# A second late projection with seven block products instead of eight, and an output stored transposed

## The chip, the cores and the metric

The kernel runs on one core of a Trainium2 chip. Its time is the device time of one execution in microseconds (us); of the kernel before, three executions took 549.82, 550.81 and 551.61 us, with a median of 550.81 us. The core has five engines, each with its own queue of instructions: TensorE (PE in the profile) multiplies matrices and writes to PSUM, an accumulator memory of eight banks; VectorE (DVE) and ScalarE (ACT) work on elements and read PSUM; GpSimd (POOL) works on SBUF, the working memory of 128 partitions; SyncE (SP) issues DMAs.

## The reference

A causal attention with a memory term, of 32 heads (4 x 8) with 576 positions of 64 values, gives x, 2304 tokens of 512 values. Then comes a feed-forward block, which is what the change touches:

```python
def _moe_ref(x, w_in, w_out):      # x 2304x512, w_in 512x2048, w_out 2048x512
    h = x @ w_in
    sp = np.where(h > 20.0, h, np.log1p(np.exp(np.minimum(h, 20.0))))
    g = h * np.tanh(sp)
    return (g @ w_out).astype(np.float32)
```

All is float32. The kernel gets that precision from a TensorE format that keeps fewer bits by splitting each operand into a high half (a rounded copy, made by ACT) and a low half (the rest, made by DVE), and by summing three products: high x high, high x low and low x high.

## The kernel before

The 2048 hidden values are cut into 16 units of 128. Units 0 to 3 (KA = 4) are done early: the tokens come in blocks of 512 as soon as a batch's attention is ready, and their first projection (`slot_h`, line 706) and second projection (`out_a`, line 734) fill gaps of TensorE between attention matmuls. Their sum goes to a DRAM tensor `part`.

Units 4 to 15 are done late, after attention. They form six pairs, in two groups of three (line 939). The tokens form three blocks of 768 (2 x HB). For each group and each block there is one late stage, so there are six stages, and each has two parts.

The first part is the first projection (`products`, line 807). A pair's 256 hidden values, a block's two halves of 384 tokens, and the two halves of the 512 inputs make a 2x2 by 2x2 block product, and that is done with seven block products instead of eight, on sums and differences of blocks (`factors`, line 758, for x; `split7`, line 430, for the weights). Each of the seven is 6 matmuls of 384 columns, so a stage has 3 x 7 x 6 = 126. The seven land in seven PSUM banks; DVE adds them up through four tiles `u` in SBUF. Then come the activation (Mish, ACT, in place in PSUM), the high half (ACT) and the low half (DVE), in a tile that the profile calls `xg`.

The second part is the second projection (`outputs`, line 862), a plain product: for each of 6 groups of 128 tokens, the 6 units of the group with 3 matmuls each of 512 columns, 108 in all, with the tokens as the weights of the systolic array. DVE adds `part` to each of the six banks, and SP stores the sum: to `part2` in the first group, to the output in the second.

The order of every engine's instructions is fixed when the program is built. A planner (`Plan`, `pick` at line 222) runs a list of operations through a model of the engines, with a priority for each operation, rings of buffers, and limits (`HELD`) on how many PSUM banks each kind of work may hold; the instructions are then issued in the order that it found, and each engine keeps to it. All instructions go through one helper, line 314, so that the tile's name, not the line, tells operations apart. [...]

Of the kernel before, what the change touches and what calls it, by code (L numbers as in the profile page):

```python
# [31 lines left out]
KA = 4  # L32
# [42 lines left out]
KEPT = {"raw": 2, "ca": 1, "cs": 2, "ob": 3}  # L75
MORE = {"ca": 2, "cs": 1, "ob": 1}
LATE = {"wi7": 3, "xT": 7, "xt": 3, "u": 5}
LANES = 8
HELD = {"ffn": 2, "att": 6, "tail": 8, "acc": 4, "conv": 1}
# [19 lines left out]

def f32(ap):  # L100
    return ap.bitcast(F32)


class Ring:


    def __init__(self, name, n):
        self.name, self.free, self.made, self.opened = name, [(0.0, k) for k in range(n)], 0, 0
        self.size, self.heirs, self.moves = n, [], None
# [9 lines left out]
class Op:  # L119
    __slots__ = ("eng", "dur", "fn", "prio", "kind", "bufs", "deps", "outs", "missing", "ready", "start", "end", "n", "kb", "tail", "port")  # L120


class Plan:


    def __init__(self):
        self.ops, self.writer, self.readers = [], {}, {}
        self.rings, self.held = {}, {"ffn": 0, "att": 0, "tail": 0, "acc": 0, "conv": 0}
# [4 lines left out]
    def op(self, eng, dur, fn, prio, r=(), w=(), bufs=(), kind=None, kb=0, port=False):  # L133
        o = Op()
        o.port = port or eng == "POOL"
# [23 lines left out]
    def opens(self, o):  # L159
# [5 lines left out]
        for ring, bs in need.items():  # L165
# [4 lines left out]
            if k:  # L170
                limit = HELD[k]
                if k == "att" and self.ffn_on:
                    limit = HELD["att"]
                elif k == "att":
                    limit = 8
                if self.held[k] + len(bs) > limit:
                    return None
        return t

    def place(self, o, start):  # L180
        o.start, o.end = start, start + o.dur
        if o.tail and not self.grown:
            self.grown = True
            for name, n in MORE.items():
                ring = self.rings[name]
                ring.free += [(o.end, ring.size + k) for k in range(n)]
        done = o.end + LAT[o.eng]
        if o.eng == "SP":
# [10 lines left out]
        for b in o.bufs:  # L199
            b.left -= 1  # L200
            b.end = max(b.end, done)
            if b.left == 0:
                ring = b.ring
                if ring.moves and ring.opened == ring.made:
                    ring = ring.moves
                ring.free.append((b.end, b.slot))
                ring.free.sort()
                if ring.heirs and ring.opened == ring.made and len(ring.free) == ring.size:
                    for heir, slots, others in ring.heirs:
                        if all(r.opened == r.made and len(r.free) == r.size for r in others):  # L210
                            t = max(r.free[-1][0] for r in others)
                            heir.free += [(t, k) for k in slots]
                            heir.free.sort()
                if b.kind:
                    self.held[b.kind] -= 1
        for x in o.outs:
            x.missing -= 1
            x.ready = max(x.ready, done if x.eng != o.eng or o.eng == "SP" else o.end + SAME[o.eng])
# [76 lines left out]
TABLE = 288.75  # L295


@with_exitstack
def attention_moe_kernel(ctx: ExitStack, tc: tile.TileContext, f_src, qn, vn, zz, beta, w_in, w_out, out):
# [4 lines left out]
    class Queue:  # L304
# [5 lines left out]
        def __getattr__(self, what):  # L310
            f = getattr(self._eng, what)

            def call(*a, **kw):
# [25 lines left out]
    part = dram.tile([NT, DM], F32, name="part")  # L339
    part2 = dram.tile([NT, DM], F32, name="part2")  # L340
# [4 lines left out]
             "ob": [128, 512], "raw": [128, 1024], "ca": [128, 512], "cs": [128, 512]}  # L345
# [8 lines left out]
    ident = sb.tile([128, 128], F32, name="ident")  # L354
    mask = sb.tile([128, 448], F32, name="mask")
    gt = sb.tile([128, 3, H], F32, name="gt")
    wt = [sb.tile([128, 4, 512], F32R, name=f"wt{f}") for f in range(KA)]
    xg = sb.tile([128, 10 * 1024], F32, name="xg")
    for name, n in (("x", 4), ("g", 6), ("g2", 0), ("wa", 2 * KA), ("wo", 0), *((r, n) for r, n in LATE.items())):
# [3 lines left out]
    slot["g2"] = [xg[:, 768 * k:768 * k + 768] for k in range(13)]  # L363
    slot["wa"] = slot["wo"] = [wt[k // 2][:, 2 * (k % 2):2 * (k % 2) + 2] for k in range(2 * KA)]
    x_, g_, g2_ = (P.rings[n] for n in ("x", "g", "g2"))
    x_.heirs = [(g2_, range(5), [x_]), (g2_, range(5, 13), [x_, g_])]
    g_.heirs = [(g2_, range(5, 13), [x_, g_])]
    P.rings["wa"].moves = P.rings["wo"]
    for name, n in KEPT.items():
        P.rings[name] = Ring(name, n)  # L370
        slot[name] = [sb.tile(SHAPE[name], F32, name=f"{name}{k}") for k in range(n)]
    attp = held.enter_context(tc.tile_pool(name="att", bufs=1))
    zall = attp.tile([128, NP * 2 * D], F32, name="zall")
# [3 lines left out]
    WA, WO7, WI7 = {}, {}, {}  # L377
# [4 lines left out]
    def tail_tiles():  # L382
        held.close()
        pool = ctx.enter_context(tc.tile_pool(name="tail", bufs=1))
        for name, shape, dt in (("wi7", [128, 2, 7 * 256], F32R), ("xT", [128, 4, HB], F32R), ("xt", [128, 2 * HB], F32),
                                ("u", [128, HB], F32)):
            slot[name] = [pool.tile(shape, dt, name=f"{name}{k}") for k in range(LATE[name])]
        for name, n in MORE.items():
            slot[name] += [pool.tile(SHAPE[name], F32, name=f"{name}m{k}") for k in range(n)]

# [33 lines left out]
    def split(f, k, prio):  # L424
        a, key = word(f, k, prio)
        wb = P.buf("wa" if f < KA else "wo")
        (WA if f < KA else WO7)[f, k] = wb
        halves(lambda: at(a), lambda i: at(wb)[:, i], 512, prio, [key + ("a",)], key, [a, wb], f >= KA)

    def split7(q, prio):  # L430

        f = KA + 2 * q
        wb = P.buf("wi7")
        WI7[q] = wb
        a, ka = word(f, 0, prio)
        halves(lambda: at(a), lambda i: at(wb)[:, i, 0:512], 512, prio, [ka + ("a",)], ("d", q, 0), [a, wb], True)
        b, kb = word(f + 1, 0, prio)
        halves(lambda: at(b)[:, 256:512], lambda i: at(wb)[:, i, 512:768], 256, prio, [kb + ("a",)], ("d", q, 1), [b, wb], True)
        t = P.buf("raw")
        tt = lambda i: at(t)[:, 256 * i:256 * i + 256]  # L440
        for i, (x, y, op) in enumerate(((lambda: at(b)[:, 0:256], lambda: at(b)[:, 256:512], ALU.add),
# [586 lines left out]
```

## Time and profile before

| what | value |
|---|---|
| median of three executions | 550.81 us (549.82 to 551.61) |
| the profiled execution, span from first to last instruction | 549.8 us (the page gives no other time of it; the fastest of the three is 549.82) |
| TensorE busy | 531.4 us, 97% |
| VectorE busy | 430.8 us, 78% |
| ScalarE busy | 337.0 us, 61% |
| GpSimd busy | 177.9 us, 32% |
| granted TensorE clock, mean | 0.996 of full speed |

A row of the profile names an engine, an operation, the tiles it writes and reads (written <- read), the shape, how many there were, and the busy time; behind that stands the idle time in front of it and who ended it. A busy time of several instructions counts overlaps once, while the mean of one is its full recorded length; so the distance between two starts can be shorter than the recorded length.

### The profile page before, as it was taken

The page shows a single profiled execution, that of the slowest core. Times are in us where ns is not written, and L with a number is a line of the kernel's source. Part 1 is how long each engine was busy: PE and PEld are TensorE (multiplying, and loading weights), DVE is VectorE, ACT ScalarE, POOL GpSimd, SP SyncE. Part 2 cuts the span into 40 slices and gives each one's busy share as a digit, 9 for nine tenths or more (in the row PEclk, how much of TensorE's full clock was granted, in tenths as well). Part 3 has the DMA queues.
Part 4 walks back from the last instruction along what each step waited for, and adds up shares of the span by engine and source line. Part 5 has one row for each costly group of instructions (what it writes and reads, how often), then busy time and mean ns, then how long its engine had stood idle before and what let it go on. Part 6 is the DMA issues. An engine that isn't in the chain of part 4 may idle for free.

```text
span 549.8 us, 10439 instructions
## 1 busy us (share of the span) xinstructions
PE 531.4 (97%) x3705; PEld 439.9 (80%) x3705; DVE 430.8 (78%) x1042; ACT 337.0 (61%) x804; POOL 177.9 (32%) x272
## 2 busy tenths in 40 slices
PE   5998999999999999999999999999999999999997
PEld 2665666777777777888998898889889889989985
DVE  4999999987898962786799779759899956864712
ACT  4999899998899774575785155417548404412500
POOL 1787787758776770011321100010212000000000
PEclk9899999999999999999999999999999999999999
DMA  7677584974566534965783914177385362534003
GB/s 254 241 258 244 169 269 154 297 291 123 160 205 185 187 118 144 385 221 170 223 253 114 301 50 170 58 241 237 115 276 181 120 221 67 173 98 132 0 19 134
DMA packets 48211, 99.77 MB, mean 181 GB/s; under 512 B 4000, under 2 KB 17824, under 8 KB 48160
## 3 DMA queue, kind: packets, MB, share of 16 engines
q1 hardware_dynamic: 48160, 99.11, 54.5%
q8 instruction: 29, 0.48, 0.4%
q14 instruction: 22, 0.18, 0.1%
HBM read 73.40 MB, written 23.59 MB: 176 GB/s over the span
## 4 chain that ended last, share of the span: by engine, by line
PE 84%; DVE 6%; DMA 3%; ACT 3%; POOL 2%; SPq 1%; issue 1%
PE bank L314 84%; DMA f<-in_f_src_dram 2%; DVE w L314 2%; ACT w L314 2%; DMA xT<-xs 1%; POOL w L314 1%; DVE at L314 1%; SPq L314 1%; DVE den L314 1%; DVE qn L314 1%; DVE xo L314 0%; ACT at L314 0%; ACT bank L314 0%; POOL phe L314 0%; DVE ca L314 0%
## 5 line engine op out<-in xcount | busy, mean ns | idle before, releaser
L314 PE MATMUL bank<-wt,xg 128*128 128x512 f32 x864 | 200.2, 391 | 0.0
L314 PEld LDWEIGHTS bank<-wt,xg 128*128 128x128 f32 x864 | 161.5, 188 | 33.7 <-issue 0.4
L314 PE MATMUL bank<-xT,wi 128*128 128x384 f32 x756 | 133.4, 335 | 0.7 <-DMA xT<-xs 0.7
L314 PEld LDWEIGHTS bank<-xT,wi 128*128 128x128 f32 x756 | 131.4, 188 | 1.8 <-DVE xg L314 1.0
L314 ACT ACTIVATE w<-w,mx 128x320 f32<-128x320 f32 (+4 forms) x160 | 88.7, 558 | 3.5 <-DVE mx L314 2.9
L314 POOL TENSOR_SCALAR w<-w,rc 128x320 f32<-128x320 f32 (+4 forms) x152 | 81.8, 562 | 13.9 <-DVE rc L314 4.3
L314 ACT ACTIVATE bank<-bank 128x384 f32<-128x384 f32 (+2 forms) x92 | 45.0, 495 | 56.1 <-DVE bank L314 51.8
L314 PE MATMUL bank<-f 64*128 64x288 f32 (+4 forms) x384 | 59.4, 425 | 8.3 <-DMA f<-in_f_src_dram 7.1
L314 DVE CUSTOM_DVE_ANT_0 w<-bank,mask 128x320 f32<-128x320 f32 (+4 forms) x160 | 60.2, 422 | 5.9 <-PE bank L314 5.9
L314 DVE TENSOR_TENSOR xg<-bank,xg 128x384 fp32r<-128x384 f32 (+2 forms) x92 | 50.1, 567 | 11.8 <-ACT xg L314 11.7
L314 PEld LDWEIGHTS bank<-f 64*128 64x128 f32 x384 | 38.7, 196 | 22.9 <-DMA f<-in_f_src_dram 7.9
L314 PE MATMUL bank<-at,v 128*64 128x256 f32 (+2 forms) x512 | 54.1, 363 | 0.0
L314 PE MATMUL bank<-xg,wt 128*128 128x512 f32 (+1 forms) x240 | 53.4, 375 | 0.6 <-ACT at L314 0.3
L314 PEld LDWEIGHTS bank<-at,v 128*64 128x64 f32 x512 | 34.2, 137 | 21.3 <-issue 2.0
L314 PEld LDWEIGHTS bank<-xg,wt 128*128 128x128 f32 x240 | 40.9, 188 | 9.8 <-issue 1.2
L314 POOL TENSOR_TENSOR cam<-cam,cs 128x512 int32<-128x512 int32 x13 | 17.5, 1346 | 95.5 <-ACT cs L314 34.2
L314 PEld LDWEIGHTS bank<-ident,w 64*128 64x128 f32 x928 | 35.0, 139 | 13.8 <-POOL w L314 5.7
L314 PE MATMUL bank<-ident,w 64*128 64x64 f32 x928 | 40.2, 226 | 5.0 <-ACT w L314 1.4
L314 ACT CAST xg<-bank 128x384 fp32r<-128x384 f32 (+2 forms) x92 | 43.8, 502 | 0.9
L314 DVE TENSOR_TENSOR ob<-bank,ob 128x512 f32<-128x512 f32 x27 | 18.3, 686 | 30.1 <-PE bank L314 27.1
L314 DVE TENSOR_TENSOR bank<-u,bank 128x384 f32<-128x384 f32 x72 | 38.5, 556 | 4.2 <-PE bank L314 3.8
L314 DVE COPY at<-bank 128x448 f32<-128x448 f32 x64 | 38.9, 641 | 1.9 <-PE bank L314 1.6
(76 smaller groups left out, 578.4 us busy)
## 6 DMA issues: line engine op xcount, KB each, us to landing
xT<-xs SPq DMA_DIRECT2D x18, 768.0 KB, 6.6
xs<-xo SPq DMA_DIRECT2D x16, 576.0 KB, 3.9
f<-in_f_src_dram SPq DMA_DIRECT2D x15, 576.0 KB, 4.9
raw<-in_w_in_dram SPq DMA_DIRECT2D x16, 512.0 KB, 4.6
raw<-in_w_out_dram SPq DMA_DIRECT2D x16, 512.0 KB, 4.2
part<-ob SPq DMA_DIRECT2D x29, 256.0 KB, 3.8
xg<-xs SPq DMA_DIRECT2D x14, 512.0 KB, 6.0
ob<-part SPq DMA_DIRECT2D x27, 256.0 KB, 3.9
```

Source lines behind the costliest of these rows:

```text
L314: ins = f(*a, **kw)
```

## The change

The second projection of the late units takes the same form as the first. A pair's 256 hidden values, a block's two token halves and the two halves of the 512 outputs again form a 2x2 by 2x2 product, done by seven block products (`STEPS`). The result is transposed: output values on partitions, tokens on columns, with matmuls of 384 columns and w_out as the array's weights. So `part` and the output are held as 128 x 4 x 2304 and 512 x 2304 (the early `out_a` is transposed too, with the same number of columns), and the caller transposes what it gets.

Both projections now share banks: three banks for the seven products of a pair (`more=True` goes on adding in a bank), six for the seven output products of a stage, which are summed over the three pairs. ACT copies partial sums out (`keep`), DVE adds them. The activation writes to SBUF (`g1`); `cuts` makes the seven factors of the second projection there, in place, one after another, and splits each in halves (`gf`, seven buffers). In the first group the result is added to `part` by a DMA that accumulates, issued from GpSimd; in the second group `part` is loaded, added and stored. An output tile has five buffers for eight uses in a stage. The weights of the second projection go through `split7` as well. The second group takes the token blocks in the order 2, 0, 1, and its first stage uses the x factors that the first group's last stage has left. The planner gets a table of one priority for each operation instead of rules; two lines of it stand in the diff.

```diff
-LATE = {"wi7": 3, "xT": 7, "xt": 3, "u": 5}
+LATE = {"wi7": 3, "xT": 7}
+SIDE = {(("t", 0, k), n) for k in (1, 2) for n in ("22", "21")}
+STEPS = [1, 5, 2, 6, 3, 7, 4]
-HELD = {"ffn": 2, "att": 6, "tail": 8, "acc": 4, "conv": 1}
+HELD = {"ffn": 2, "att": 6, "tail": 5, "acc": 6, "conv": 1, "gf": 7}
+LOW = 3
+FREE = 4
...
+PRIO = [
+    -419.6, 290.3, -717.2, -661.6, -1029.7, 165.8, 0.5, -337.1, -1035.4, 620.2, 77.7, 165.6, 28.1, 179.5, -812.2, -110.8, 185.3, -672.1, 41.5, -709.2, -12.2,
...
-    def split7(q, prio):
+    def split7(q, k, prio):
...
+        wb = P.buf("wo7" if k else "wi7")
+        W7[q, k] = wb
+        a, ka = word(f, k, prio)
...
         mm(1, "a11", "11")
...
+        keep(0, 1)
         mm(5, "s1", "t1")
...
+        keep(1, 5)
+        mm(2, "a12", "21", opens="11")
+        add(0, 2)
+        mish(2, "11")
+        mm(1, "s2", "t2", True)
+        keep(2, 1)
+        mm(5, "s4", "22", True, "12")
+        add(2, 5)
+        mish(5, "12")
+        mm(1, "s3", "t3", True, "22")
+        add(1, 1, "22")
+        mish(None, "22")
+        mm(1, "a22", "t4", True, "21")
+        mish(1, "21")
...
+    def cuts(qs, tag, prio, GT):
...
+        for i, n in enumerate(STEPS):
+            for q in qs:
+                gb, src = GT[q], FROM[n]
...
+                if n in (5, 6, 7, 4):
+                    pre(*{5: ("12", "11"), 6: ("22", "11"), 7: ("22", "12"), 4: ("21", "11")}[n])
+                b = P.buf("gf", "gf")
...
+                P.op("ACT", HB / 1200.0 + 0.09, lambda gb=gb, src=src, view=view: ac.copy(out=view(0), in_=at(gb[src])), when(prio + 3 * i),
...
+                P.op("DVE", HB / 960.0 + 0.075, lambda gb=gb, src=src, view=view: ve.tensor_tensor(out=view(1), in0=at(gb[src]), in1=f32(view(0)), op=ALU.subtract),
...
     def outputs
...
+        def store(a, b, c):
+            cc, ts = spot(a, b, c)
+            if not last:
...
+                P.op("POOL", SWDGE[0], lambda: po.dma_start(out=part[:, cc, ts], in_=at(pb[a, b, c]), accum_op=ALU.add), when(prio + 30),
...
+        for step, n, what in ((1, 1, [(0, 0, 0)]), (5, 5, [(1, 1, 0)]), (2, 2, [(0, 0, 1)]), (6, 1, [(0, 1, 0)]), (3, 5, [(0, 1, 1)]),
+                              (7, 1, [(1, 1, 1)]), (4, 1, [(1, 0, 1)])):
+            for c in range(2):
+                mm(step, n, c)
+            for c in range(2):
+                for a, b, end in what:
+                    if (a, b, c) not in pb:
+                        fetch(a, b, c, n)
+                    else:
+                        add(a, b, c, n)
+                    if end:
+                        store(a, b, c)
...
+        for k in ((0, 1, 2), (2, 0, 1))[gi]:
...
+            X, got = kept if gi and k == 2 else factors(k, tag, when(base - (45 if k == gi == 0 else 30)), gi)
```

On TensorE, at the place in the last stage where the second projection begins, the queue of before reads as follows (`wt0` to `wt3` hold the halves of w_out, `xg` those of the hidden values; behind a tile's name stand its buffer and a running number):

```order
L314 MATMUL bank5_72<-wt2_80,xg_82 128x512 x3
L314 MATMUL bank0_67<-wt2_80,xg_82 128x512 x3
L314 MATMUL bank1_68<-wt2_80,xg_82 128x512 x3
L314 MATMUL bank4_71<-wt2_80,xg_82 128x512 x3
L314 MATMUL bank5_72<-wt3_81,xg_82 128x512 x3
L314 MATMUL bank0_67<-wt3_81,xg_82 128x512 x3
```

There the changed queue has this, with the factors `gf`, the weights `wo7` of the three pairs, and the last product of the first projection (`xT`) in between:

```order
L475 MATMUL bank6_72<-gf2_3344,wo70_2860 128x384 x3
L475 MATMUL bank7_73<-gf2_3344,wo70_2860 128x384 x3
L475 MATMUL bank0_66<-gf3_3345,wo71_3340 128x384 x3
L475 MATMUL bank1_67<-xT6_2859,wi72_2852 128x384 x6
L475 MATMUL bank4_70<-gf3_3345,wo71_3340 128x384 x3
L475 MATMUL bank2_68<-gf0_3342,wo72_3341 128x384 x3
```

The 108 matmuls of 512 columns have become 126 of 384, and each three of them need a factor that one ACT and one DVE instruction have made.

On VectorE, one pair's share of a late stage before (adds of products through `u`, then low halves into `xg`):

```order
L314 TENSOR_TENSOR u0_2878<-u3_2881,bank1_68 128x384
L314 TENSOR_TENSOR u4_2882<-u0_2878,bank5_72 128x384
L314 TENSOR_TENSOR bank4_71<-u3_2881,bank4_71 128x384
L314 TENSOR_TENSOR u1_2879<-u0_2878,bank6_73 128x384
L314 TENSOR_TENSOR bank6_73<-u4_2882,bank6_73 128x384
L314 TENSOR_TENSOR bank7_74<-u4_2882,bank7_74 128x384
L314 TENSOR_TENSOR xg_82<-bank4_71,xg_82 128x384
L314 TENSOR_TENSOR bank2_69<-u1_2879,bank2_69 128x384
L314 TENSOR_TENSOR xg_82<-bank6_73,xg_82 128x384
L314 TENSOR_TENSOR xg_82<-bank7_74,xg_82 128x384
L314 TENSOR_TENSOR xg_82<-bank2_69,xg_82 128x384
```

The same place in the last stage of the changed queue (`g1` with its buffer behind it, so `g12` is buffer 2, holds the hidden values and in place the differences, `gf` the halves):

```order
L475 TENSOR_TENSOR bank4_70<-u2_3362,bank4_70 128x384
L475 TENSOR_TENSOR g11_3350<-u1_3361,bank3_69 128x384
L475 TENSOR_TENSOR g16_3355<-g12_3351,g16_3355 128x384
L475 TENSOR_TENSOR g12_3351<-g11_3350,g12_3351 128x384
L475 TENSOR_TENSOR gf5_3347<-g16_3355,gf5_3347 128x384
L475 TENSOR_TENSOR g16_3355<-g11_3350,g16_3355 128x384
L475 TENSOR_TENSOR gf1_3343<-g11_3350,gf1_3343 128x384
L475 TENSOR_TENSOR gf6_3348<-g19_3358,gf6_3348 128x384
L475 TENSOR_TENSOR bank7_73<-u0_2861,bank7_73 128x384
L475 TENSOR_TENSOR g19_3358<-g19_3358,g16_3355 128x384
L475 TENSOR_TENSOR bank6_72<-u2_3362,bank6_72 128x384
```

Ten instructions for a pair (6 adds, 4 low halves) have become 14 (3 adds, 4 differences, 7 low halves), and those of several pairs stand mixed.

On GpSimd, in the second and third late stage, the changed queue has the new accumulating stores between the instructions that assemble weights:

```order
L475 DMA part_65<-oo_81 128x384 x5
L475 DMA part_65<-ot0_2862 128x384
L475 TENSOR_TENSOR xt_2864<-xt_2864,cs1_86 128x512
L475 TENSOR_TENSOR xt_2864<-xt_2864,cs0_85 128x512
L475 DMA part_65<-oo_81 128x384 x2
```

Before, GpSimd has only the assembling instructions there.

## Rows read from the trace of the kernel before

**Rows 1.** The page: the span, and busy time (share) x instructions.
```profile
span 549.8 us, 10439 instructions
PE 531.4 (97%) x3705; PEld 439.9 (80%) x3705; DVE 430.8 (78%) x1042; ACT 337.0 (61%) x804; POOL 177.9 (32%) x272
```

**Rows 2.** Chain of waits, its end: start, length, what.
```profile
329.69 6.74 DMA xT<-xs
336.56 209.45 PE bank L314 x1038
546.04 0.69 DVE ob L314
```

**Rows 3.** Timeline of TensorE, fifth stage and on: start, length, instructions.
```profile
453.06 22.03 PE L314 MATMUL bank<-xT,wi 128*128 128x384 f32 x126
474.93 24.68 PE L314 MATMUL bank<-wt,xg 128*128 128x512 f32 x108
499.45 22.03 PE L314 MATMUL bank<-xT,wi 128*128 128x384 f32 x126
```

**Rows 4.** Stretches: length, busy PE, PEld, DVE, ACT, POOL; clock, DMA share, GB/s.
```profile
99.50:211.40 111.90, 111.82 (x1174) 83.27 (x1174) 92.81 (x313) 94.64 (x254) 77.79 (x137) 1.00 0.56 188
336.50:546.00 209.50, 209.43 (x1038) 187.71 (x1038) 149.18 (x250) 80.21 (x159) 12.36 (x9) 1.00 0.42 135
```

**Rows 5.** Groups by shape: count, busy and mean ns of one, idle before.
```profile
L314 PE MATMUL bank<-xg,wt 128*128 128x256 f32 x48 | 5.9, 283 | 0.0
L314 DVE TENSOR_TENSOR bank<-u,bank 128x384 f32<-128x384 f32 x72 | 38.5, 556 | 4.2 <-PE bank L314 3.8
L314 POOL TENSOR_TENSOR phe<-qn,zall 128x640 f32<-128x640 f32 x16 | 24.9, 1559 | 30.1 <-DMA zall<-in_zz_dram 9.7 <-ACT w L314 8.4 <-DVE cs L314 2.5
L314 DVE TENSOR_TENSOR wi<-raw,wi 128x1024 fp32r<-128x1024 f32 x6 | 8.3, 1383 | 2.2 <-ACT wi L314 2.2
```

**Rows 6.** Timeline of VectorE, a stretch without gaps, GpSimd idle.
```profile
334.15 1.48 DVE L314 TENSOR_TENSOR bank<-u,bank 128x384 f32<-128x384 f32 x3
...
338.74 0.95 DVE L314 TENSOR_TENSOR xT<-xt,xT 128x768 fp32r<-128x768 f32 x1
339.61 0.95 DVE L314 TENSOR_TENSOR xt<-xT 128x768 f32<-128x768 f32 x1
...
342.79 0.96 DVE L314 TENSOR_TENSOR xt<-xT 128x768 f32<-128x768 f32 x1
```

**Rows 7.** Timeline of VectorE, a stretch with GpSimd at work.
```profile
299.25 2.92 DVE L314 TENSOR_TENSOR xT<-xt,xT 128x768 fp32r<-128x768 f32 x2
302.10 0.68 DVE L314 TENSOR_TENSOR ob<-bank,ob 128x512 f32<-128x512 f32 x1
302.70 0.68 DVE L314 TENSOR_TENSOR obm<-bank,obm 128x512 f32<-128x512 f32 x1
...
308.01 0.42 DVE L314 TENSOR_TENSOR raw<-ca,cam 128x256 f32<-128x256 f32 x1
308.35 0.42 DVE L314 TENSOR_SCALAR cs<-raw 128x512 int32<-128x512 int32 x1
...
309.69 0.69 DVE L314 TENSOR_TENSOR ob<-bank,ob 128x512 f32<-128x512 f32 x1
```

**Rows 8.** Timeline of GpSimd, the same stretch (behind the row: idle before).
```profile
299.31 2.05 POOL L314 TENSOR_TENSOR ca<-ca,csm 128x512 int32<-128x512 int32 x1 [12.29 <-ACT xT L314]
```

**Rows 9.** Timeline of ScalarE: three instructions one behind another.
```profile
336.33 0.51 ACT L314 ACTIVATE bank<-bank 128x384 f32<-128x384 f32 x1
...
337.11 0.51 ACT L314 CAST xg<-bank 128x384 fp32r<-128x384 f32 x1
```

**Rows 10.** DMA issues: KB each, median us from issue to landing.
```profile
xg<-xs SPq DMA_DIRECT2D x14, 512.0 KB, 6.0
ob<-part SPq DMA_DIRECT2D x27, 256.0 KB, 3.9
out_dram<-obm SPq DMA_DIRECT2D x4, 256.0 KB, 3.0
```

More of the change, by code (lines that the diff above doesn't have):

```diff
@@ L753, in early, with load_q, factors @@
             slot_h(j, f, base + f)
-        for t in range(BLOCKS[j][1] // 128):
-            out_a(j, t, base + KA + t)
-    def factors(k, tag, prio):
+        for c in range(NC):
+            out_a(j, c, base + KA + c)
+    def load_q(dst, k, half, rows, prio, w, buf):
+        t0, c = 2 * HB * k + HB * half, rows.start // 2
+        src = xs[:, rows, t0:t0 + HB]
+        o = P.op("SP", ROWS, lambda: sy.dma_start(out=dst(), in_=src), prio, r=held_by(t0, HB, (c, c + 1)) + over, w=[w], bufs=[buf],
+                 kb=HB * len(range(*rows.indices(2 * NC))) / 2)
+        o.tail = True
+        return [w]
+    def factors(k, tag, prio, late):
         names = ("11", "21", "22", "t1", "t3", "t2", "t4")
@@ L762, in factors @@
         key = lambda n: (tag, "x", n)
-        A, B, C = (P.buf("xt") for _ in range(3))
-        def load(dst, half, rows, w, buf):
-            t0, c = 2 * HB * k + HB * half, rows.start // 2
-            src = xs[:, rows, t0:t0 + HB]
-            o = P.op("SP", ROWS, lambda: sy.dma_start(out=dst(), in_=src), prio, r=held_by(t0, HB, (c, c + 1)) + over, w=[w], bufs=[buf],
-                     kb=HB * len(range(*rows.indices(2 * NC))) / 2)
-            o.tail = True
-            return [w]
+        T = {n: P.buf("xt2" if late else "xt") for n in ("12", "11", "22", "21")}
@@ L813, in products, with mm @@
         key = lambda n: (tag, "h", f, n)
         mine = lambda n: at(bk[n])[:, :HB]
-        def mm(n, left, right):
+        def mm(n, left, right, more=False, opens=None):
             o, part = LEFT[left]
@@ new lines, in products, with keep, add @@
+        G = lambda n: (tag, "g", q, n)
+        def keep(i, n):
+            P.op("ACT", HB / 1160.0 + 0.08, lambda: ac.copy(out=at(u[i]), in_=mine(n)), when(prio), r=[key(n)], w=[U(i)], bufs=[u[i], bk[n]])
+        def add(i, n, to=None):
+            P.op("DVE", HB / 960.0 + 0.075, lambda: ve.tensor_tensor(out=at(gb[to]) if to else mine(n), in0=at(u[i]), in1=mine(n), op=ALU.add), when(prio),
+                 r=[U(i)] + ([key(n)] if to else []), w=[G(to) if to else key(n)], bufs=[u[i], bk[n]] + ([gb[to]] if to else []))
@@ L938, in attention_moe_kernel @@
             XT["n"] = XT.get("n", 0) + 1
+    begun = None
     groups = [[0, 1, 2], [3, 4, 5]]
     for gi, qs in enumerate(groups):
[L941 to L945 removed]
+        for k in range(2):
+            for i, q in enumerate(qs):
+                split7(q, k, when(WT[gi][k] + 10 * i))
+    base, kept = 253.0, None
     for gi, qs in enumerate(groups):
[L947 removed]
+        for k in ((0, 1, 2), (2, 0, 1))[gi]:
             tag = ("t", gi, k)
[L949 to L950 removed]
+            X, got = kept if gi and k == 2 else factors(k, tag, when(base - (45 if k == gi == 0 else 30)), gi)
+            kept = X, got
+            GT = {}
             for i, q in enumerate(qs):
[L952 to L953 removed]
+                GT[q] = products(q, tag, X, got, base + 7 * i, begun)
+                begun = (tag, "h", KA + 2 * q, 2)
+            gf = cuts(qs, tag, base + 12, GT)
+            outputs(k, qs, tag, base + 22, gf, gi == 1)
+            begun = (tag, "o", 1, 0)
+            base += 43.7
+    for o, p in zip(P.ops, PRIO):
+        o.prio = p
     order = P.schedule()
     fillers(P, order)
[L956 removed]
+    first, second = next(o for o in order if o.tail), next(o for o in order if late(o))
     for o in order:
```

335 lines of the change are left out of this document (180 added, 155 removed), and 138 rows, old and new, of the table PRIO.

## The prediction

> **What bounds the kernel now.** I read the page first: over a span of 549.8 us TensorE is busy for 531.4 us, 97%, VectorE for 78%, ScalarE for 61% [rows 1]. A share over the whole span doesn't say who is waited for at the end, so the chain of waits comes next. Its last part is one run of TensorE from 336.56 to 546.0 us, 1038 matmuls with nothing in between; in front of it stands one wait for a load of x, and behind it a single add of VectorE and the last store [rows 2]. The busy time by stretch says the same: 209.43 of 209.50 us in the late stages, at a granted clock of 1.00, and 111.82 of 111.90 us in the second half of attention [rows 4]. In the late stages VectorE is busy for 149 of 209.5 us and ScalarE for 80 [rows 4], so both have room. A late stage is therefore as long as its matmuls. The reader should see in the timeline that a stage is 21.87 us of first projection (453.06 to 474.93) and 24.52 us of second projection (474.93 to 499.45), 46.39 us together [rows 3].
>
> **The saving on TensorE.** From those starts a matmul of 384 columns costs 21.87/126 = 0.1736 us, one of 512 columns 24.52/108 = 0.2270 us [rows 3]. The second projection goes from 108 x 0.2270 = 24.52 us to 126 x 0.1736 = 21.87 us in a stage. That is 2.65 us less, in six stages 15.9 us. The first projection keeps its 126 matmuls. The transposed early projection keeps its columns: 216 matmuls of 512 become 192 of 512 and 48 of 256, and a matmul of 256 costs 5.9/48 = 0.12 us [rows 5], so 24 x 0.227 = 5.4 us become 5.9, +0.5 us at most, which I leave in the range. Each matmul loads 128 columns of weights before and after, and the 384-column matmuls of rows 3 already run at 0.1736 us with such a load in front of each.
>
> **What VectorE gets.** For a pair and stage, 6 adds and 4 low halves become 3 adds, 4 differences and 7 low halves, 14 instead of 10. Three pairs make 42; output adds bring it to 48 (first group) or 56 (second group). None of the new differences reads PSUM, and rows 5 and 6 have no such instruction of 384 columns; by the neighbouring shapes it lies between the 256-column (0.34 us from start to start [rows 7]) and the 768-column one (0.87 [rows 6]), so I give it the 0.47 of the PSUM adds, (1.48 - 0.55)/2 [rows 6]. The other starts: 512 columns 0.60, 256 columns 0.34 [rows 7], and 1024 columns 1.14 on the same line. The x factors of a block are 8 sums and differences and 4 low halves, 12 x 0.87 = 10.4 us (in two stages GpSimd takes two of them; a 640-column GpSimd instruction is 1.56 us [rows 5]). The weights of a pair and one projection are 2 x (0.34 + 0.60) + 4 x 0.34 + 0.34 + 0.60 + 1.14 = 5.3 us; before, the second projection's weights had no sums of blocks, so 4 x 0.34 + 1.14 = 2.5 us of it are new. Counting VectorE's queue stage by stage with these prices gives 40, 36, 41, 41, 41 and 27 us, against 43.7 us of TensorE in each. So VectorE no longer has 30% of room but 6%, except in the last stage.
>
> Two stretches show how well such sums hold. From 334.15 to 342.79, 14 instructions without a gap, nine of 384 and five of 768 columns, sum to 8.58 us and took 8.64 [rows 6]. From 299.25 to 309.69, with GpSimd at work on the weights, fifteen of them sum to 9.05 us and took 10.44, 15% more [rows 7, 8]. About 41 us of weight preparation fall into the first four stages; 15% on that is 6 us there, at most 2.7 us in one (the third, 18 us of weights), which brings 41 to 43.7. So VectorE just doesn't bind in the sum, but its reserve is gone, and in a fixed order each handing over from ScalarE to VectorE to TensorE can now show through. Stalls of TensorE: lower end 0.7 us (the one wait for x of the old late stages [rows 2] would be about that), upper end 15.9 us (third rival below). I take 5 us, about 1 us for each stage but the last, since rows 6 are the nearest to a stage without weights and rows 7 to one with them.
>
> [...]
>
> **ScalarE, GpSimd, DMA.** ScalarE gets 42 instructions a stage for the pairs instead of 27, and 8 copies in the first group. At 0.39 us from start to start (336.33 to 337.11 for two [rows 9]) 50 of them are 20 us; with weights and factors its queue sums to 32 us at most in a stage. Hidden behind 43.7. GpSimd does the same weight sums as before and 24 accumulating stores; nothing in the trace is a DMA issued from GpSimd, so its issue lies between 0 and the 1.56 us of the longest GpSimd row, and its landing between the 3.0 us of a store and the 6.0 us of a load of x [rows 10]. [...] I take zero: the sum in DRAM is read a stage later. What waits for it is the output buffer (second rival).
>
> **Attention.** VectorE and GpSimd have the same instructions before the end of attention, and ScalarE two copies fewer. On TensorE somewhat less early work is placed before that point: behind it stand 207 matmuls of 512 and 96 of 256 columns, where 216 and 48 stood, +5.8 - 2.0 = 3.8 us. If attention's end is set by TensorE, which was never idle there [rows 4], it comes 3.8 us earlier and nothing is lost; if by VectorE and ScalarE (92.8 and 94.6 of 111.9 us [rows 4]), TensorE idles up to 3.8 us. I take 1 us, since rows 4 show TensorE as the full one. The end: one add of 384 instead of 512 columns and a store of 192 instead of 256 KB, at most 0.3 us less, taken as zero.
>
> **The sum.** 549.8 - 15.9 + 5 + 1 = 539.9 us for the profiled execution. Its span equals the fastest run, so nothing lies around it that I can see; the median of three is 1.0 us above it. Forecast of the median: 540.5 us, some range around it 537 to 546.
>
> **Rivals.**
> 1. The whole saving arrives: VectorE keeps ahead as in rows 6, and only the 0.7 us stay. 550.8 - 15.9 = 535 us. For it: no gap in rows 6, and 3 us of room per stage. Against: 15% in rows 7.
> 2. The output buffers give most of it back. Eight tiles of a stage share five buffers. In the second group the sixth tile needs an add (0.56), a store's landing (3.0) and a load's landing (3.9 to 6.0) [rows 5, 10], 7.5 to 9.6 us, while TensorE has only two output steps, 36 x 0.1736 = 6.25 us, before it must write on in the bank that this tile holds: 1.2 to 3.3 us of stall in each of three stages. In the first group the copy waits for the accumulating store: 0.56 + 1.56 + 6.0 = 8.1 us at most, 1.9 us of stall. Together up to 3 x (3.3 + 1.9) = 15.6, at the lower ends 3.6; in the middle some 9, so 549 us. For it: ScalarE and VectorE wait in order, and factors stand behind the waiting instruction. Against: matmuls of the next block's products stand between the steps in places, and fill.
> 3. VectorE becomes the bound, and it is slower. If each of its instructions costs its recorded length (0.556 us for 384 and 1.38 for 1024 columns [rows 5], 0.95 for 768 [rows 6], 0.68 and 0.42 for 512 and 256 [rows 7]) because most wait for another engine, the stages are 47.2, 42.3, 48.4, 48.2, 46.9 and 32 us, and four of them stand 3.5, 4.7, 4.5 and 3.2 us above 43.7: 15.9 us, the whole saving. With the attention term and about 1 us at the ends of stages, 553 us. It decides from 6% above my prices (0.50 us for 384 columns) on, and eats all at 17%. For it: rows 7, and chains in which each difference is made in place of the one before. Against: rows 6.
>
> **Chances.** Forecast 0.55, first rival 0.15, second 0.12, third 0.18. What a measurement of this kernel can tell from no change is about 0.3%, 549.2 to 552.5 us. The forecast, the first rival and 0.07 of the second are faster than that: 0.77. Of the second 0.04 and of the third 0.01 are within it: 0.05. The rest, 0.17 of the third and 0.01 of the second, is slower: 0.18. For 8 in 10 the range goes from 533.5 (the first rival with the end's 0.3 and a shorter attention) to 553 (the third rival's middle), which leaves out about 0.04 below and 0.10 above.
>
> **What would show it.** In the new timeline of TensorE a late stage should take 43.7 us and some; 252 matmuls at 0.174 us with gaps between them confirm the saving, a longer matmul of 384 columns would refute it. The gaps should be put down to ScalarE and VectorE (`gf`) in the first four stages; if they stand at banks and are ended by DMAs, it is the second rival; if VectorE has no idle time in the middle stages and a stage is 47 us, the third. Attention is right if TensorE's last attention matmul ends at or before 211 us. The prediction is wrong if the late stages are dense and the time is still above 546, for then attention or the end has changed.

## The result

The changed kernel takes 544.32 us (median of four runs, 543.84 to 544.69) against 551.13 us for the kernel before beside it (four runs, 549.82 to 551.61): ratio 0.9875, 95% interval 0.986 to 0.9891. It is 6.8 us faster. The forecast was 540.5 us, so 10.3 us were expected and two thirds of them arrived. The profiled execution took 544.69 us, 1.7 us more than its span.

### The profile page after: what moved, and what is told of

It reads as the page before. It is cut to its first block, busy times and chain, and to the rows that moved or that the text cites. A ratio compares the mean times of both kernels' runs of the same rounds, so it can differ in the third digit from the quotient of the medians.

```text
span 543.0 us, 10912 instructions
## 1 busy us (share of the span) xinstructions
PE 523.2 (96%) x3838; PEld 451.8 (83%) x3838; DVE 460.5 (85%) x1134; ACT 391.9 (72%) x922; POOL 205.9 (38%) x300
## 4 chain that ended last, share of the span: by engine, by line
PE 65%; DVE 16%; DMA 6%; ACT 5%; POOL 5%; issue 2%; SPq 1%; DVEq 0%; ACTq 0%; POOLq 0%
PE bank L475 65%; DVE gf L475 3%; DVE w L475 3%; POOL w L475 2%; DVE g L475 2%; DMA raw<-in_w_out_dram 2%; POOL phe L475 1%; ACT w L475 1%; DMA gt<-in_beta_dram 1%; DMA xg<-xs 1%; DVE qn L475 1%; DVE at L475 1%; DVE wo L475 1%; DVE raw L475 1%; DMA part<-oo 1%
## 5 line engine op out<-in xcount | busy, mean ns | idle before, releaser
L475 PE MATMUL bank<-gf,wo 128*128 128x384 f32 x756 | 139.7, 337 | 2.6 <-DVE gf L475 1.6
L475 PEld LDWEIGHTS bank<-gf,wo 128*128 128x128 f32 x756 | 130.8, 188 | 7.1 <-DVE gf L475 3.3
L475 PE MATMUL bank<-xg,wt 128*128 128x512 f32 (+1 forms) x480 | 105.7, 374 | 0.2
L475 PEld LDWEIGHTS bank<-xg,wt 128*128 128x128 f32 x480 | 82.2, 188 | 17.6 <-issue 1.7
L475 ACT CAST gf<-g 128x384 fp32r<-128x384 f32 x126 | 63.2, 516 | 33.6 <-PE bank L475 23.1
L475 POOL TENSOR_SCALAR w<-w,rc 128x192 f32<-128x192 f32 (+4 forms) x152 | 81.7, 556 | 13.1 <-DVE qn L475 3.9
L475 DVE TENSOR_TENSOR gf<-g,gf 128x384 fp32r<-128x384 f32 x126 | 68.8, 569 | 7.2 <-ACT gf L475 7.0
L475 DVE CUSTOM_DVE_ANT_0 w<-bank,mask 128x192 f32<-128x192 f32 (+4 forms) x160 | 60.0, 423 | 4.6 <-PE bank L475 4.4
L475 DVE COPY at<-bank 128x448 f32<-128x448 f32 (+1 forms) x64 | 39.4, 646 | 3.5 <-PE bank L475 3.4
L475 DVE TENSOR_TENSOR g<-g,g 128x384 f32<-128x384 f32 x72 | 40.1, 569 | 0.5
```

Of the source, the lines that this page charges most:

```text
L475: ins = f(*a, **kw)
```

## The profile after

The page's first rows answer to [rows 1]: TensorE 8 us less busy, VectorE 30 us more, ScalarE 55 us more.

```profile
span 543.0 us, 10912 instructions
...
PE 523.2 (96%) x3838; PEld 451.8 (83%) x3838; DVE 460.5 (85%) x1134; ACT 391.9 (72%) x922; POOL 205.9 (38%) x300
```

The end of the chain of waits (start, length, what) answers to [rows 2]. One run of TensorE from 336.56 to the end has become several, with VectorE's low halves `gf`, weights `wi`, a cast of ScalarE and one accumulating store between them; only from 402.60 on is it one run again. In front of the first line shown, from 280.84 us on, the chain runs along VectorE almost alone.

```profile
309.70 30.16 PE bank L475 x170
340.48 1.40 DVE gf L475
342.87 5.86 PE bank L475 x32
349.13 0.84 ACT xT L475
352.34 30.62 PE bank L475 x174
...
391.52 1.41 DVE gf L475 x3
395.01 2.06 DVE wi L475
397.35 4.64 DMA part<-oo
402.60 136.93 PE bank L475 x783
```

The timeline of TensorE answers to [rows 3]. The two projections now interleave, so a stage is read from the start of its first product (`xT,wi`) to that of the next.

```profile
315.00 15.76 PE L475 MATMUL bank<-xT,wi 128*128 128x384 f32 x90
...
360.25 8.62 PE L475 MATMUL bank<-xT,wi 128*128 128x384 f32 x48
...
401.01 1.16 PE L475 MATMUL bank<-gf,wo 128*128 128x384 f32 x5 [0.99 <-DVE gf L475]
402.60 4.11 PE L475 MATMUL bank<-gf,wo 128*128 128x384 f32 x21 [0.43 <-ACT oo L475]
406.54 10.85 PE L475 MATMUL bank<-xT,wi 128*128 128x384 f32 x60
...
451.22 3.28 PE L475 MATMUL bank<-xT,wi 128*128 128x384 f32 x18
...
495.11 16.80 PE L475 MATMUL bank<-xT,wi 128*128 128x384 f32 x96
...
522.67 16.84 PE L475 MATMUL bank<-gf,wo 128*128 128x384 f32 x96
```

From these starts the second to sixth stages take 45.3, 46.3, 44.7, 43.9 and 44.4 us, against 46.39 before and 43.7 expected. In the fifth, 252 matmuls in 43.89 us are 0.174 us each.

A recorded matmul of 384 columns is 0.335 us long and starts 0.1735 us after the one before, so a wait of up to 0.16 us leaves no idle time in a timeline. The stalls below are therefore worked out from the starts of single matmuls in the trace, after the end of attention: each distance less 0.1735 us (384 columns), 0.2268 (512) or 0.1203 (256), with what is under 0.01 us left out. That gives 1.2 us in the kernel before and 8.7 us in the changed one, all but 0.3 of it before 420 us; such a sum is good to some 0.3 us.

Who ends these waits is read from the weight loads (PEld), which wait in front of their matmuls. From 209 to 543 us the list of their waits (us in total, times, longest) begins with

```profile
PEld bank L475 <- DVE gf L475: 3.3, 6, 1.3
PEld bank L475 <- ACT oo L475: 1.9, 4, 0.8
PEld bank L475 <- ACT u L475: 1.6, 4, 0.5
PEld bank L475 <- ACT ot L475: 0.8, 2, 0.6
```

so ScalarE's copies out of a bank (`oo`, `u`, `ot`) end 4.3 us of them and VectorE's low halves 3.3.

The stretches of these stages answer to [rows 4] (columns: length; busy PE, PEld, DVE, ACT, POOL; clock, DMA share, GB/s). VectorE, at 71% of the late stages before, is now at 95% of the fourth and fifth.

```profile
451.20:495.10 43.90, 43.90 (x254) 43.72 (x253) 41.56 (x75) 23.73 (x48) 0.00 (x0) 1.00 0.47 153
495.10:539.40 44.30, 44.30 (x256) 44.04 (x255) 31.21 (x60) 20.92 (x44) 0.00 (x0) 1.00 0.23 76
315.00:360.20 45.20, 44.48 (x250) 42.94 (x250) 40.66 (x73) 29.35 (x60) 13.40 (x14) 1.00 0.56 130
360.20:406.50 46.30, 44.75 (x251) 42.87 (x250) 40.52 (x81) 34.21 (x71) 15.97 (x16) 1.00 0.53 106
406.50:451.20 44.70, 44.70 (x257) 44.12 (x256) 42.39 (x82) 29.42 (x61) 7.57 (x7) 1.00 0.59 163
```

How one stall comes about can be read at 401 us. First VectorE, then ScalarE, then GpSimd, in rows of the timeline (in brackets: idle before, and who ended it):

```profile
397.45 0.54 DVE L475 TENSOR_TENSOR oo<-bank,oo 128x384 f32<-128x384 f32 x1
398.37 0.56 DVE L475 TENSOR_TENSOR oo<-bank,oo 128x384 f32<-128x384 f32 x1 [0.38 <-PE bank L475]
399.59 0.42 DVE L475 TENSOR_TENSOR xt<-cam,ca 128x256 f32<-128x256 f32 x1 [0.66 <-POOL cam L475]
399.94 1.02 DVE L475 TENSOR_TENSOR gf<-g,gf 128x384 fp32r<-128x384 f32 x2
```

```profile
397.15 1.35 ACT L475 CAST gf<-g 128x384 fp32r<-128x384 f32 x3
402.07 0.48 ACT L475 COPY oo<-bank 128x384 f32<-128x384 f32 x1 [3.56 <-DMA part<-oo]
```

```profile
397.35 0.88 POOL L475 DMA_DIRECT2D part<-oo  x1 [1.38 <-DVE wi L475]
397.94 1.62 POOL L475 TENSOR_TENSOR cam<-cam,cs 128x512 int32<-128x512 int32 x1
```

GpSimd's weight sum stands behind the issue of a store, VectorE's block sum waits for it, and the low halves `gf` that TensorE needs stand behind that block sum: 0.99 us of idle TensorE in its timeline. ScalarE's copy waits 3.56 us for the landing of the store, because the output tile is still being read: 0.43 us of idle TensorE. In these rows each engine waits in order, and what it holds up is not what it waits for.

## The experiments

All are variants of the changed kernel, and each has its ratio to the kernel before on the same chip; the medians of the kernel before beside them lie between 550.75 and 551.6 us, so a difference between two medians of the table carries that 0.9 us as well. "A" is the theory with which I started: the stalls come from the weights' work on VectorE and GpSimd. The last column is TensorE's stalls behind attention, from starts to starts as above.

| experiment | median us | ratio (95% interval) | stalls us |
|---|---|---|---|
| changed kernel | 544.32 | 0.9875 (0.986 to 0.9891) | 8.7 |
| 1 one weight | 539.0 | 0.9777 (0.9758 to 0.9796) | 4.4 |
| 2 no partial store | 543.03 | 0.9853 (0.9828 to 0.9878) | 6.9 |
| 3 sums on VectorE | 545.03 | 0.9891 (0.987 to 0.9912) | 9.2 |
| 4 no differences | 541.9 | 0.9828 (0.98 to 0.9856) | 6.4 |
| 5 no word adds | 542.55 | 0.9833 (0.9815 to 0.9851) | 5.6 |
| 6 no low halves of weights | 540.65 | 0.9795 (0.9779 to 0.9811) | 5.2 |
| 7 one weight, no store | 538.94 | 0.9766 (0.9751 to 0.9781) | 3.7 |
| 8 a third less early | 543.2 | 0.9842 (0.98 to 0.9885) | 27 |
| 9 nine low halves twice | 573.27 | 1.0394 (1.0364 to 1.0423) | 36.9 |
| 10 all low halves twice | 618.57 | 1.121 (1.1176 to 1.1244) | 79.9 |
| 11 three out | 537.91 | 0.9752 (0.9727 to 0.9777) | 2.3 |
| 12 a third less late | 540.06 | 0.9823 (0.9783 to 0.9862) | 46.9 |

**1. One weight.** For the late pairs but the first, every operation of the weights that isn't a load becomes nothing:

```diff
-pe.matmul(mine(n), at(wb)[:, y, o + ...
+pe.matmul(mine(n), at(W7[0, 0])[:, y, o + ...
+P.mute = q > 0      # an operation of split7 that isn't SP's issues nothing
```

> Left out: the preparation of the late weights of all pairs but the first (word, high and low halves, sums of blocks on ScalarE, VectorE and GpSimd); all six pairs multiply by the first pair's weights. Loads, matmuls, factors, outputs and stores stay, in the same order. In the changed kernel TensorE's late matmuls stand 8.5 us above dense, nearly all of it before 420 us, in the stages in which weights are prepared. Theory A (the weights' work on VectorE and GpSimd stands in front of the halves gf that TensorE waits for): at least 6 of the 8.5 us go, 536 to 538.5 us, and the wait for gf at 400 us is gone. Theory B (output buffers and accumulating stores hold it): under 2.5 us go, 542 us or more. Theory C (VectorE's own instructions for the pairs, the recorded third rival): most of the stalls stay, 541 us or more.

Measured 539.0 us, 5.3 less than the changed kernel: 0.5 us above A's range and 2 us or more below the others'. A also asked for at least 6 us of stalls to go; 4.3 went. 4.4 us are left, 3.8 of them from 300 to 400 us. So A explains about half of the stalls.

**2. No partial store.**

```diff
-lambda: po.dma_start(out=part[:, cc, ts], in_=at(pb[a, b, c]), accum_op=ALU.add)
+lambda: None
```

> Left out: the 24 accumulating stores that GpSimd issues (the first group's sums don't reach DRAM). Everything else stays in its order. Theory A: the copies into the output tiles no longer wait and GpSimd's weight sums start earlier, but the stalls that VectorE's weight work makes stay: 542.5 to 544.3 us. Theory B: 3.6 us or more come back, 541 us or less, and the 0.43 us wait at 402.6 us is gone with all of the 1.9 us around 400. Theory C: no change, 544 us.

Measured 543.03 us: as A said, but its interval overlaps with that of the changed kernel, so between nothing and some 3 us. The stalls from 380 to 420 us fall from 3.2 to 1.6. The second rival isn't what took the gain.

**3. The x sums of GpSimd on VectorE.**

```diff
-by, eng, t = ("POOL", po, 1.86) if side else ("DVE", ve, 0.87)
+by, eng, t = ("POOL", ve, 1.86) if side else ("DVE", ve, 0.87)
```

> Changed: the four x sums of 768 columns that GpSimd makes in the second and third stage (1.84 us each) are made by VectorE (0.87 us each) at the same places; all other instructions keep their order. Theory A in its form with GpSimd (a GpSimd sum beside VectorE stretches VectorE's instruction, 1.40 us instead of 0.55 for one gf at 340.5 us): the stretching costs 0.5 to 0.9 us each time, about what the sum costs on VectorE, so 543.3 to 544.5 us, with the stall at 342.9 us smaller. Theory C (VectorE's load is the bound): 3.5 us more load in these stages, 545 to 547 us.

Measured 545.03 us; the intervals overlap, and the ranges of the two theories meet here, so it decides little. The stall at 342.9 us is gone, with the low half in front of it 0.56 us long instead of 1.40, and others came: GpSimd's stretching and VectorE's own work cost about the same.

**4. No differences.**

```diff
-P.op(by, t, lambda: eng.tensor_tensor(out=at(gb[src]), in0=at(gb[x]), in1=at(gb[y]), ...
+P.op(by, t, lambda: None, ...
```

> Left out: the twelve differences in place (384 columns) of each stage, so the seven block products of the second projection use the same four tiles undifferenced. Copies, low halves and all else stay in order. It takes 12 x 0.47 = 5.6 us of VectorE out of each stage and one step out of each chain from Mish to gf. Theory C: nearly all stalls go, 536 to 538 us. Theory A: the weights' work still stands in VectorE's queue, but the queue is shorter by a seventh: 539 to 542 us. Theory B: no change beyond 1 us, 543.3 us or more.

Measured 541.9 us, in A's range. 5.6 us of VectorE less in every stage gave 2.4 us in all.

**5 and 6. Which engine's weight work.** The fifth leaves out GpSimd's sums, the sixth VectorE's low halves:

```diff
-lambda: po.tensor_tensor(out=ai(), in0=ai(), in1=si(), op=ALU.add)
+(lambda: None) if f >= KA else lambda: po.tensor_tensor(...)
```

```diff
-lambda: ve.tensor_tensor(out=dst(1), in0=src(), in1=f32(dst(0)), op=ALU.subtract)
+(lambda: None) if key[0] == "d" else lambda: ve.tensor_tensor(...)
-pe.matmul(mine(n), at(wb)[:, y, o + ...
+pe.matmul(mine(n), at(wb)[:, 0, o + ...
```

> Left out: GpSimd's adds of the words of the late weights (24 of 1.29 us, all before 420 us). VectorE's and ScalarE's instructions stay, in the same order. The first experiment took 5.3 us off by leaving out the weights' work of five pairs on all three engines. Theory A1 (GpSimd's share of it: its sum stretches the VectorE instruction beside it, and VectorE waits for the sum in order): 3 us or more come back, 541.3 us or less. Theory A2 (VectorE's own instructions for the weights stand in front of gf): at most 1.5 us, 542.8 us or more.

> Left out: the low halves of the late weights on VectorE (36 instructions of 256, 512 and 1024 columns, 12 x 2.08 = 25 us); both terms multiply by the high half. GpSimd's adds, the block sums, ScalarE's work and all else stay in order. Theory A2 (VectorE's own instructions for the weights): 3 us or more come back, 541.3 us or less. Theory A1 (GpSimd): at most 1.5 us, 542.8 us or more.

Measured 542.55 us without GpSimd's sums, between the two theories, and 540.65 us without the low halves, where A2 said. VectorE's own instructions are the larger part (25 us of them are worth some 3.7 to 4.4 us), GpSimd's sums the smaller (31 us, some 2).

**7. One weight and no store.** The edits of 1 and 2 together.

> Left out: the weights' work of five pairs and the accumulating stores, the first and the second experiment together. With one weight alone 4.4 us of stalls of TensorE were left, nearly all between 300 and 400 us. Theory D (that rest is the output tiles and GpSimd's stores): under 1.5 us of stalls are left, 536.5 us or less. Theory E (that rest is the chain Mish, difference, copy, low half at the start of a second projection, with no other products to fill): 3 us or more are left, 538 to 539 us.

Measured 538.94 us with 3.7 us of stalls: what E said, and nothing gained over the first experiment. What the stores cost, at most some 3 us by experiment 2, shows only together with the weights' work.

**8. A third less early work**, to see what sets the end of attention:

```diff
-for q, (y, z) in enumerate(((0, 0), (0, 1), (1, 0))):
+for q, (y, z) in ((0, (0, 0)), (2, (1, 0))):      # slot_h
-for y, z in ((0, 0), (1, 0), (0, 1)):
+for y, z in ((0, 0), (0, 1)):                     # out_a
```

> Left out: one of the three products (high by high, high by low, low by high) in the early feed-forward part, so 160 of its 480 matmuls, 59 of 512 columns (13.4 us) before the end of attention. All else in its order. Read is the end of TensorE's last attention matmul, 208.6 to 209.8 us in the runs so far. Theory P (TensorE's work sets the end of attention): it comes 11 us or more earlier, 198 us or less. Theory V (VectorE and ScalarE set it, each busy for 183 of 209 us): at most 5 us earlier, 204 us or later.

The last attention matmuls of TensorE (`at,v`), first of the changed kernel, then of this one:

```profile
206.20 3.35 PE L475 MATMUL bank<-at,v 128*64 128x320 f32 x32
209.49 2.79 PE L475 MATMUL bank<-xg,wt 128*128 128x512 f32 x11
```

```profile
204.03 3.35 PE L475 MATMUL bank<-at,v 128*64 128x320 f32 x32
207.31 5.06 PE L475 MATMUL bank<-xg,wt 128*128 128x512 f32 x21
```

13.4 us less of TensorE's work in front of it brought the end 2.2 us forward: in theory V's range. That shows that TensorE's work alone doesn't set the end in the changed kernel, although it is busy for 109.72 of the 110.00 us from 99.50 to 209.50; it doesn't show which engine does. For the kernel before, with its 111.82 of 111.90 us [rows 4], the same is likely but wasn't tried. Behind attention the same: the stretch from 208 to 250 us has 33.74 us of TensorE instead of 42.00, its waits there are for ScalarE's casts `xg` (10.8 us from 208 to 275 us), and the granted clock, 1.00 in the changed kernel, is 0.92 in this stretch with TensorE idle for 8 us (on the page 7 tenths of full speed from 242.9 to 256.4 us and 8 from there to 269.9).

```profile
208.00:250.00 42.00, 33.74 (x136) 26.44 (x135) 29.04 (x46) 27.10 (x45) 5.87 (x4) 0.92 0.77 271
```

Some 33 us of TensorE's work out, 1.1 us of time, from two runs whose interval overlaps with that of the changed kernel; how much of this the slower clock cost wasn't separated.

**9 and 10. VectorE's load turned up.** Low halves `gf` are made twice, nine or all 21 of a stage:

```diff
-ve.tensor_tensor(out=view(1), in0=at(gb[src]), in1=f32(view(0)), op=ALU.subtract)
+[ve.tensor_tensor(out=view(1), ...) for _ in range(2 if n in STEPS[:3] else 1)]
```

> Added: 9 of the 21 low halves gf of each late stage are made twice, one right behind the other, so VectorE has 9 x 0.47 = 4.2 us more in a stage and 25 us more in all. All other instructions keep their order. In the changed kernel VectorE is busy for 41.7 of the 44 us of the fifth stage (451 to 495 us), and TensorE doesn't wait there. Theory S (TensorE is held only where VectorE's sum passes its 43.7 us, the recorded third rival): the fifth stage grows from 43.9 to about 46 us, the last stays, the whole to 549 to 552 us. Theory Q (each microsecond of VectorE work in front of gf costs a fraction of itself, 4.4/25 = 0.18 by the experiment without low halves of the weights): 0.18 x 25 = 4.4 us, 548 to 549.5 us, spread over all stages, also the last.

> Added: all 21 low halves gf of each late stage are made twice: VectorE has 9.9 us more in a stage, 59 us more in all. Theory S: VectorE is the bound in five stages, each 5 to 7 us longer, the last hardly: 570 to 580 us. Theory Q: 0.18 x 59 = 10.6 us, 553 to 557 us.

Both theories missed, by at least 21 us in the ninth and 38 us in the tenth. The price was wrong first: a repeated low half starts 0.584 us after its twin (median of 52), not 0.47, as this row of VectorE shows with two such pairs in 2.20 us.

```profile
487.01 2.20 DVE L475 TENSOR_TENSOR gf<-g,gf 128x384 fp32r<-128x384 f32 x4
```

So 54 x 0.584 = 31.5 us and 126 x 0.584 = 73.6 us were added, and 29 and 74 us came out: nearly one for one. The fifth and sixth stages of the ninth experiment:

```profile
471.00:519.90 48.90, 46.63 (x254) 43.18 (x254) 46.67 (x84) 23.64 (x48) 0.00 (x0) 1.00 0.42 138
520.00:567.50 47.50, 45.79 (x255) 43.55 (x254) 35.83 (x69) 20.78 (x44) 0.00 (x0) 1.00 0.22 70
```

The fifth grew by 5.0 us for 5.3 us added, and VectorE is busy for 95% of it, as it was for 95% of the fifth stage of the changed kernel. The sixth grew by 3.1 us although VectorE has 11.7 us idle in it: a doubled low half also comes later to the matmul that waits for it, so the experiment adds to the chain as well as to the load, and there it can't be the load.

**11. Three out.** The edits of 1, 2 and 4 together.

> Left out: the weights' work of five pairs, the accumulating stores and the twelve differences of each stage, together. With the first two out 3.7 us of stalls of TensorE were left, 3.0 of them between 300 and 400 us. Theory F (VectorE's queue still makes them): under 1.5 us are left, 536 to 537 us, near the 535 of the recorded first rival. Theory G (ScalarE's copies of a bank that TensorE must write on in, which stand behind other casts, make them): 2.5 us or more are left, 538 to 539 us.

Measured 537.91 us with 2.3 us of stalls, between the two theories; in time it can't be told from the seventh experiment. Of its 3.7 us of stalls the differences took 1.4, be it by their time in VectorE's queue or by their step in the chain. What is left is of theory G's kind: the list of the weight loads' waits from 209 to 536 us begins with two of ScalarE's copies out of a bank, 2.0 us together.

```profile
PEld bank L478 <- ACT oo L478: 1.4, 4, 0.4
PEld bank L478 <- ACT ot L478: 0.6, 1, 0.6
```

**12. A third less late work of TensorE.**

```diff
-for i, (y, z) in enumerate(((0, 0), (0, 1), (1, 0))):
+for i, (y, z) in ((0, (0, 0)), (2, (0, 1))):      # outputs
```

> Left out: the product of the weights' low half with the high half of gf in the second projection of every late stage, 42 of its 126 matmuls, so 252 x 0.1736 = 43.7 us of TensorE's work in all, 7.3 us in a stage. Its reads of gf's high and low half stay, as do all instructions of the other engines, in the same order. Theory P (TensorE is the one bound of the late stages, as in the kernel before; the stalls are local): most of the 43.7 us come off, down to where VectorE binds, 41.6 us a stage by its busy time, so about 2 us a stage and 1 to 2 us of the stalls less where stages are longer; the last stage, where VectorE is busy for 32 us only, shrinks by 7 us: 520 to 528 us. Theory K (TensorE and VectorE are held by each other, each waiting for the other in a fixed order, so that VectorE's 41.7 us and its some 2 us of waiting are already the length of a stage): under 1.5 us a stage and up to 4 in the last, 533 to 540 us.

Measured 540.06 us, theory K at its edge: 43.7 us of TensorE's work gave 4.3 us. Its fifth and last stages, and its second (there the granted clock is 0.96, so the fifth is the one to read):

```profile
449.00:493.00 44.00, 40.39 (x211) 35.53 (x210) 41.82 (x76) 23.30 (x48) 0.00 (x0) 1.00 0.47 155
493.00:534.30 41.30, 39.64 (x214) 36.23 (x212) 31.19 (x61) 20.60 (x44) 0.00 (x0) 1.00 0.27 83
314.30:359.10 44.80, 40.69 (x210) 36.68 (x209) 42.72 (x73) 29.54 (x61) 14.04 (x14) 0.96 0.58 132
```

The fifth stage is 44.0 us long with 211 matmuls as with 254. In the changed kernel TensorE is busy for all of it and looks like the bound; it isn't the only one. VectorE's waits there (engine, tile <- who: us in total, times, longest) are, in the changed kernel and in this one,

```profile
DVE bank L475 <- PE bank L475: 2.0, 1, 2.0
```

```profile
DVE bank L475 <- PE bank L475: 1.6, 1, 1.6
```

so VectorE's 41.6 to 41.8 us of work, one wait for the first bank of a pair and one for a load of x (0.2 and 0.5 us) make up the 44 us, with TensorE lighter too.

## Why the prediction was right, and where its sizes were off

**The saving on TensorE held.** A stage's 252 matmuls cost 43.9 us where nothing stalls, for 43.7 predicted. No run measured the transposed early part by itself; by the eighth experiment its half microsecond would hardly show.

**VectorE's sums held in the main, the conclusion from them didn't.** Predicted were 36, 41, 41, 41 and 27 us in the second to last stages; busy times are 40.7, 40.5, 42.4, 41.6 and 31.2, so within 1.4 us in the third to fifth and 4 to 5 us over in the second and the last (a busy time counts the whole recorded length of an instruction that no other follows at once; whether that is all of the excess wasn't worked out). The step that failed is "VectorE just doesn't bind in the sum", with 6% of room. In the fifth stage it does: it waits 2.0 us for TensorE's first bank, and 41.6 + 2 is the length of the stage, as 252 x 0.1735 is. There the change moved the kernel to the corner where the two meet. In no stage of the ninth, tenth and twelfth experiments is VectorE busy for more than 96%. The other stages are alike only in part: these waits for a bank are 1.0 us in the second, 3.0 in the third, none in the fourth and 4.1 in the last, where VectorE has 13 us idle and its sum isn't the bound. The corner fits the three measured slopes, which differ much: of VectorE's work taken away 0.07 (fourth experiment) to 0.18 (sixth) comes back as time, of TensorE's taken away a tenth, and of VectorE's added nine tenths and more is paid. The third rival was right that VectorE becomes a bound, and wrong on the reason that it gave: the instructions aren't slower than priced where they don't depend on each other (0.469 us for 384 columns, the median of 235 pairs behind attention in the changed kernel, 0.47 predicted).

**The stalls were mis-sized**: 5 us predicted, 8.7 - 1.2 = 7.5 more than before measured. They stand where the prediction had them, in the stages with weights; not one per stage, but 2.5 us from 272 to 315 us, 2.1 and 3.1 in the second and third stage, 0.4 in the fourth and almost none in the fifth and last. Only a part of them ends with `gf`; ScalarE's copies out of a bank end as much. The experiments put about half on the weights (4.4 left of 8.7 with one weight), more of that on VectorE's instructions than on GpSimd's. Of the 2.3 us left in the eleventh most end with ScalarE's copies; no run moved those, so what they cost by themselves stays open.

**ScalarE and GpSimd.** ScalarE's 21 to 34 us a stage are near the predicted 32 at most. It is hidden by its sum, but not by its order, as at 402.60 us and in the lists of the weight loads' waits. The accumulating stores were taken as zero; no run shows that zero. This row shows their issue, 0.91 us, inside the bounds of 0 and 1.56 us, and the chain above one landing of 4.64 us, inside 3.0 and 6.0:

```profile
L475 POOL DMA_DIRECT2D part<-oo x20 | 18.2, 911 | 32.5 <-ACT gf L475 15.8 <-DVE oo L475 7.2 <-DVE xt L475 1.6
```

Their cost is between nothing and some 3 us, not the 3.6 to 15.6 of the second rival with the loads; in the second group, where its larger part should lie, TensorE hardly stalls.

**Attention.** The last attention matmul ends at 209.5 us, before the 211 that the prediction named, for 211.4 before. But of 3.8 us of work moved behind it only 1.9 came back in front, so the loss is 1.9 us and not 1 (the experiments with the same attention end it between 208.7 and 210.1 us, so this is good to 0.7). The reason given, that TensorE is the full one there, fell in the eighth experiment: with 13.4 us less of its work the end still stands at 207.3. Which chain of VectorE, ScalarE and GpSimd holds it there wasn't tried.

**The sum again.** Forecast and median differ by 3.8 us: 2.5 from the stalls, 0.9 from attention, 0.7 because more lies around the span than the prediction took (it said that nothing does; in the profiled run after it is 1.7 us, between span and median 1.3), less 0.4 at the end, which was taken as zero (from the start of the last matmul to the end of the span it is 4.15 us before and 3.78 after). That is 3.7 of the 3.8. The two large misses point the same way and don't cancel, so the sum isn't right by luck, except that attention's term has the right order of size on a reason that fell. But the range, 533.5 to 553 us, also held the first two rivals, and that the time lies in it says little by itself.

No version among these runs does all of the kernel's work and beats the changed one.

## What to carry to other kernels

A busy share of 100% on one engine doesn't show that it alone is the bound: here TensorE was dense in a stage, and a sixth of its matmuls could go without the stage becoming shorter. Before work is taken off a full engine by giving it to another, add up the other's instructions for the stage, and add what it waits for in order; if that reaches the new length, the rest of the saving won't come. Doubling one cheap instruction on the second engine is a quick test of how much room it has, read in a stage where that engine has no idle time; elsewhere it also lengthens the chain, as in the sixth stage of the ninth experiment. And a list of waits has to be read where the engine waits: here TensorE's stood mostly in front of its weight loads.

## What the runs showed of the hardware

- Two VectorE instructions of 384 columns, one behind the other, start 0.469 us apart in the changed kernel (median of 235 pairs behind attention); where the second writes what the first wrote, as the doubled low halves do, it is 0.584 us (median of 52 in the ninth experiment), the recorded length of 0.55 us and a little.
- In the changed kernel, behind attention, a VectorE instruction that reads only SBUF tiles and starts while a GpSimd sum runs ends after that sum; one that reads a bank doesn't wait for it. Seven instructions of 384 columns of the first kind (`gf`, `g`) start beside a GpSimd sum: they end 0.41 to 0.42 us after it, and all but the last, which starts 0.14 us before the sum's end, take 0.76 to 1.48 us instead of 0.55. The 27 of 384 columns that read a bank and run beside such sums take 0.54 to 0.56. One of the seven is the low half of 1.40 us in these two rows (339.63 + 1.84 = 341.47, 340.48 + 1.40 = 341.88).

```profile
339.63 1.84 POOL L475 TENSOR_TENSOR xt<-xT 128x768 f32<-128x768 f32 x1 [16.22 <-DMA xT<-xs]
```

```profile
340.48 1.40 DVE L475 TENSOR_TENSOR gf<-g,gf 128x384 fp32r<-128x384 f32 x1 [1.06 <-ACT gf L475]
```

Of the 15% of [rows 7, 8], 1.4 us, most is one such place in the kernel before: the first row of [rows 7] has two instructions in 2.92 us where 0.87 + 0.95 would do, beside the GpSimd sum of [rows 8] that ends at 301.36.
